# Banded attention on one Trainium2 core: normalising inside the split into two fp16 parts, tile by tile

## The chip, the cores and the metric

The program runs on one core of a Trainium2 chip. The metric is the device time of one execution in microseconds (us). In this text PE is TensorE's matmul and PEld its weight load, DVE is VectorE, ACT is ScalarE, POOL is GpSimd, and SP is the engine that issues the DMAs. "L335" is line 335 of the kernel before.

## What is computed

Three stages follow one another: an attention with a band of 128 keys and 4 "sink" keys, a feed-forward block with a three-tap convolution as its gate, and a mixing block with two token matrices. The change lies in the attention.

```python
scores = scale * np.matmul(q, k.transpose(0, 1, 3, 2))      # 2 batches, 8 heads, 768 x 768, head_dim 64
keep = is_sink | in_window                                  # 4 sinks, window 128
scores = np.where(keep, scores, -1000000000.0)
a = np.exp(scores - np.max(scores, axis=-1, keepdims=True))
a = a / (np.sum(a, axis=-1, keepdims=True) + 1e-09)
return np.matmul(a, v)
...
h = np.maximum(x @ w_in, 0.0)                               # d_model 512 -> d_ff 1024
gate = 1.0 / (1.0 + np.exp(-conv_out))                      # conv over 3 tokens
x = h * gate @ w_out
...
theta = x @ w_theta                                         # then cos, sin, two 768 x 768 token products
```

## The kernel before

**Units of work.** `body` walks through four units, one for each batch and half of the 768 query rows. A unit has four pairs of heads (`Unit.pair`), and each pair calls `head` twice. That makes 32 heads of three query tiles of 128 rows. For each tile TensorE multiplies queries and keys into PSUM (`scores`, tile `ps_s`, two buffers), VectorE adds the mask and takes the row maximum in one instruction (L315, into `e`), and ScalarE takes the exponential in place and sums it (L319). A tile of `e` is 260 columns wide: 128 keys, 4 sinks, 128 keys; the very first tile of a sequence is 128 wide. VectorE then forms the reciprocals `ri` of the three sums (L322, L323).

**Normalising and splitting.** Four heads (table `NORM`) are transposed by TensorE; the change does not touch them. The other 28 go this way. ScalarE multiplies each tile of `e` by its row factor, in place (L335). ScalarE copies the normalised blocks into fp16, the first part (L345), and VectorE subtracts that from `e` and writes the rest as a second fp16 part (L346); both go into the buffer `pb`, of which there are three. In a second half one instruction covers all three tiles (768 columns); in a first half the 128-wide tile goes alone and the other two together (512 columns). GpSimd splits the four sink columns in the same way (L349, L350). One transposing DMA, issued by SP, turns the head's parts into `pt` (L353), four buffers.

```python
for i in range(3):
    n = P if half == 0 and i == 0 else 2 * P + NS
    nc.scalar.activation(e[:, i, :n], e[:, i, :n], AF.Copy, scale=ri[:, i : i + 1])
```

**What uses it.** `pair_out` multiplies the parts in `pt` with the values, also split into two fp16 parts (`ps_o`, L411). It runs one head behind: `flush` comes after the next pair's first head. `store_x` scales the result and splits it again into `xg_hi` and `xg_lo` (L431, L432).

**What runs beside it.** Between the pairs `body` decodes the feed-forward weights (L100 to L103, L82, L84) and computes feed-forward blocks (`Group.blocks`), as the tables `CHUNKS` and `BLOCKS` say. A block is 24 matmuls into `ps_h` (L124 to L126), two ReLUs (L632), two first taps (L634), four further taps on VectorE (L636), one tanh (L640), a product (L641), a split into `ghi` and `glo` (L82, L84) and 12 matmuls into `ps_x` (L651, L652, L657). There are 24 such blocks; those that do not fit in the attention follow after it.

**What sets the order.** Each engine takes its instructions strictly in turn, and so does the DMA queue of SP. The order in these queues is written by the framework's scheduler when the program is built, from the instructions and their dependences; the tables only set the order in which they are handed to it.

Of the kernel before, what the change touches and what calls it, by code (L numbers as in the profile page):

```python
# [8 lines left out]
F32 = mybir.dt.float32  # L9
# [4 lines left out]
AF = mybir.ActivationFunctionType  # L14
ALU = mybir.AluOpType
PSUM = bass.MemoryType.PSUM

P = 128
B, H, S, D = 2, 8, 768, 64
NS = 4  # L20
SR = 3 * 3 * NS
KW = P + NS
# [23 lines left out]
RAW2 = 5  # L46
MIXED = (0, None, 1, None, None, None)
FLAG = 3
SK = 'gpsimd'
WT = 8  # L50
PRE_STACK = 1
TOK_CUT = 2
# [235 lines left out]
def scores(tc, c, half, qk, i, a):  # L288
    nc = tc.nc
    t = 3 * half + i  # L290
    ps = c.ps_s.tile([P, 512], F32, name="ps_s")
    o = KW * (max(t - 1, 0) - 2 * half)
    if len(qk) == 3:
        n = 2 * P + NS
        for k in qk[1:]:
            nc.tensor.matmul(ps[:, :n], qk[0][:, i * P : (i + 1) * P], k[:, o : o + n], start=k is qk[1], stop=k is qk[2])
        return ps
    n = P if t == 0 else 2 * P + NS
    nc.tensor.matmul(ps[:, :n], qk[0][:, a, i * P : (i + 1) * P], qk[1][:, o : o + n], start=True, stop=True)  # L299
    return ps  # L300


def head(tc, c, half, a, qk, norm):

    nc = tc.nc
    e = c.e.tile([P, 3, 2 * P + NS], F32, name="e")
    mx = c.st.tile([P, 3], F32, name="mx")
    sm = c.st.tile([P, 3], F32, name="sm")
    ri = c.st.tile([P, 3], F32, name="ri")
    for i in range(3):  # L310
        t = 3 * half + i
        n = P if t == 0 else 2 * P + NS
        ps = scores(tc, c, half, qk, i, a)
        m = c.masks[min(t, 2)]
        nc.vector.tensor_tensor_reduce(  # L315
            out=e[:, i, :n], in0=ps[:, :n], in1=m, scale=-1.0 / math.sqrt(D), scalar=3.0e38,
            op0=ALU.add, op1=ALU.min, accum_out=mx[:, i : i + 1],
        )
        nc.scalar.activation(  # L319
            e[:, i, :n], e[:, i, :n], AF.Exp, bias=mx[:, i : i + 1], scale=-1.0, accum_out=sm[:, i : i + 1]  # L320
        )
    nc.vector.tensor_scalar(sm, sm, 1.0e-9, 1.0 / SP, ALU.add, ALU.mult)  # L322
    nc.vector.reciprocal(ri, sm)  # L323
    c.last_sum = ri[:, 0:1]

    if norm == PE:
        return transposed_by_pe(tc, c, e, ri)
    nb = 5 if half == 0 else 6
    s0 = 2 if half == 0 else 0
    ns = 3 - s0  # L330
    pr = c.pbuf[c.npb % len(c.pbuf)]
    c.npb += 1
    for i in range(3):
        n = P if half == 0 and i == 0 else 2 * P + NS
        nc.scalar.activation(e[:, i, :n], e[:, i, :n], AF.Copy, scale=ri[:, i : i + 1])  # L335
    sk = e[:, s0:, P:KW]
    for i0, i1 in [(0, 3)] if half else [(0, 1), (1, 3)]:
        d0, d1 = max(2 * i0 - (1 - half), 0), 2 * i1 - (1 - half)
        hi, lo = pr[:, d0:d1, :], pr[:, nb + d0 : nb + d1, :]
        if d1 == 1:  # L340
            src, hi, lo = e[:, 0, :P], hi[:, 0, :], lo[:, 0, :]
        else:
            src = two_blocks(e, i0, i1 - i0)
            hi, lo = (x.rearrange("p (i w) q -> p i w q", w=2) for x in (hi, lo))
        nc.scalar.activation(hi, src, AF.Copy)  # L345
        nc.vector.tensor_tensor(lo, src, hi, ALU.subtract)  # L346

    ps = pr[:, 2 * nb, s0 * 3 * NS : SR].rearrange("p (i g w) -> p i g w", g=3, w=NS)
    getattr(nc, SK).tensor_copy(ps[:, :, 0:3:2, :], sk.unsqueeze(2).to_broadcast([P, ns, 2, NS]))  # L349
    getattr(nc, SK).tensor_tensor(ps[:, :, 1, :], sk, ps[:, :, 0, :], ALU.subtract)  # L350
    pt = c.pt.tile([P, 13, P], F16, name="pt")
    n = 2 * nb + 1
    nc.sync.dma_start_transpose(out=pt[:, :n, :], in_=pr[:, :n, :].rearrange("p a q -> p (a q)"))  # L353
    return pt


def transposed_by_pe(tc, c, e, ri):

    nc = tc.nc
    d = c.ma.tile([P, 3, P], F32, name="h")
    for i in range(3):
        nc.scalar.activation(d[:, i, :], c.ident, AF.Copy, scale=ri[:, i : i + 1])
    pt = c.pt.tile([P, 13, P], F16, name="pt")
    banks = c.ps_x.tile([P, DM], F32, name="ps_x"), c.ps_h.tile([P, 512], F32, name="ps_h")
    blocks = ((0, 0), (1, 0), (1, KW)), ((2, 0), (2, KW), (2, P))
    for n in range(2):
        for j, (i, k) in enumerate(blocks[n]):
            nc.tensor.matmul(banks[n][:, j * P : (j + 1) * P], e[:, i, k : k + P], d[:, i, :], start=True, stop=True)  # L370
        src = banks[n][:, : 3 * P]
        hi, lo = (pt[:, 6 * x + 3 * n : 6 * x + 3 * n + 3, :].rearrange("p a q -> p (a q)") for x in range(2))
        nc.scalar.activation(hi, src, AF.Copy)
        nc.vector.tensor_tensor(lo, src, hi, ALU.subtract)
    return pt


def two_blocks(e, i, n):

    a = e[:, i, 0 : 2 * P + NS]  # L380
    (pstep, pn), (step, _) = a.ap[0], a.ap[-1]
    return bass.AP(a.tensor, a.offset, [[pstep, pn], [(2 * P + NS) * step, n], [KW * step, 2], [step, P]])
# [65 lines left out]
class Unit:  # L448
# [11 lines left out]
    def pair(self, p):  # L460
        tc, c, b, half = self.tc, self.c, self.b, self.half
        n = (2 * b + half) * CC + p
        stack = n >= 3 * CC
        if not stack:
            while len(c.loaded) <= (n + AHEAD if n + AHEAD < 2 * CC else min(n + 1, 3 * CC - 1)):
                c.loaded.append(load_qk(tc, c, len(c.loaded)))
            qk = c.loaded[n]
        pts = []
        for a in range(2):
            if stack:  # L470
                while len(c.stacked) <= min(2 * n + a + 1, 8 * CC - 1):
                    c.stacked.append(load_stack(tc, c, len(c.stacked)))
                qk = c.stacked[2 * n + a]
            pts.append(head(tc, c, half, a, qk, NORM[n][a]))
            if n == 3 * CC - 1 and a == PRE_STACK:
                c.stacked.append(load_stack(tc, c, 3 * H))
            if a == LAG - 1:
                self.flush()
        while len(c.vp_t) <= min(p + V_AHEAD, CC - 1):
            c.vp_t.append(values(tc, c, b, len(c.vp_t)))  # L480
        c.late.append((b, p, half, pts, *c.vp_t[p]))
        if LAG == 0:
            self.flush()
# [507 lines left out]
```

## Time and profile before

| what | us |
|---|---|
| three runs | 475.7, 479.04, 496.11 |
| their median | 479.04 |
| the profiled execution, its own time | 475.81 |
| its span, first to last instruction | 474.0 |

A row of grouped instructions gives line, engine, operation, tiles (written<-read), shape and type, and the count; then the busy time in us and the mean duration of one in ns; then the idle time of the engine just before them and what ended it. Overlapping instructions count once in the busy time, so it can be less than count times mean. [...] A row of waits gives the engine and what it was to do, what ended the wait, the us in total, how often, and the longest. A row of the timeline gives start, length, engine, line, operation and, at its end, how many instructions it holds.

### The profile page before, as it was taken

To read this page: it belongs to the slowest core of one execution; us is meant where nothing else is said; L and a number is where in the kernel's file an instruction comes from. 1 tells how busy PE (TensorE), PEld (TensorE's weight loads), DVE (VectorE), ACT (ScalarE), POOL (GpSimd) and SP (SyncE) were. 2 spreads that over 40 slices of the span, in tenths; PEclk is the share of its full clock that TensorE was granted. 3 is DMA by queue.
4 is the path that set the end of the run, shared out by engine and by line. 5 is a ranking of instruction groups with operands and counts; after the bars stand their busy time and mean duration, and the time that the engine had idled before them with its cause. 6 is when DMAs were issued, how large, how long until landed. Compare 5 with 4: busy or idle time off the path is not lost.

```text
span 474.0 us, 7252 instructions
## 1 busy us (share of the span) xinstructions
PE 418.8 (88%) x2376; PEld 341.0 (72%) x2376; DVE 337.1 (71%) x870; ACT 316.2 (67%) x773; POOL 23.2 (5%) x92
## 2 busy tenths in 40 slices
PE   2877648797699899799999999899889999999994
PEld 1665336685488778688898888588668888888873
DVE  5689979997578997875699877897389973211132
ACT  2999869999999999985686877966475431100010
POOL 4101001010100101100000000000000000000000
PEclk9997778899979989899999999999989999999998
DMA  4888998567984665360434100131016730000012
GB/s 109 250 198 201 281 256 206 130 168 143 189 145 86 148 139 113 73 99 12 152 114 121 60 0 1 45 90 44 0 51 197 232 100 22 24 22 24 22 44 75
DMA packets 74589, 51.94 MB, mean 110 GB/s; under 512 B 59696, under 2 KB 63280, under 8 KB 74544
## 3 DMA queue, kind: packets, MB, share of 16 engines
q1 hardware_dynamic: 74544, 51.40, 43.6%
q8 instruction: 21, 0.34, 0.3%
q14 instruction: 24, 0.20, 0.1%
HBM read 33.95 MB, written 3.15 MB: 78 GB/s over the span
## 4 chain that ended last, share of the span: by engine, by line
PE 61%; ACT 15%; DVE 10%; DMA 9%; issue 3%; SPq 1%; POOL 0%; DVEq 0%; ACTq 0%
PE ps_y L125 7%; PE ps_y L124 7%; PE ps_y L126 7%; DMA pt<-pb 5%; PE ps_x L651 4%; PE ps_m L126 4%; PE ps_m L125 4%; PE ps_m L124 4%; PE ps_x L652 4%; PE ps_x L657 3%; PE ps_h L124 3%; PE ps_h L126 3%; PE ps_h L125 3%; ACT e L335 3%; ACT e L319 3%
## 5 line engine op out<-in xcount | busy, mean ns | idle before, releaser
L299 PE MATMUL ps_s<-qk 128*128 128x260 f32 (+1 forms) x144 | 48.7, 450 | 19.8 <-POOL sink_rows L221 8.7
L124 PE MATMUL ps_h<-xg_hi,win_hi 128*128 128x258 f32 x192 | 58.5, 306 | 1.8 <-ACT h L632 1.8
L124 PE MATMUL ps_y<-z_hi,wt_hi 128*128 128x512 f32 x144 | 57.6, 400 | 1.3 <-ACT z_hi L82 0.9
L125 PE MATMUL ps_y<-z_hi,wt_lo 128*128 128x512 f32 x144 | 57.0, 397 | 0.1
L126 PE MATMUL ps_y<-z_lo,wt_hi 128*128 128x512 f32 x144 | 56.4, 396 | 0.0
L125 PE MATMUL ps_h<-xg_hi,win_lo 128*128 128x258 f32 x192 | 55.9, 292 | 0.0
L126 PE MATMUL ps_h<-xg_lo,win_hi 128*128 128x258 f32 x192 | 55.7, 296 | 0.0
L82 ACT ACTIVATE xt_hi<-ps_t 128x512 fp32r<-128x512 f32 x24 | 13.9, 595 | 61.4 <-PE ps_t L685 61.4
L315 DVE CUSTOM_DVE_ANT_0 e<-ps_s,m 128x260 f32<-128x260 f32 (+1 forms) x96 | 37.6, 400 | 17.6 <-PE ps_s L299 12.1
L636 DVE SCALAR_TENSOR_TENSOR cv<-h,cw_t,cv 128x256 f32<-128x256 f32 x96 | 44.5, 480 | 7.4 <-ACT cv L634 6.8
L319 ACT ACTIVATE e<-e,mx 128x260 f32<-128x260 f32 (+1 forms) x96 | 47.7, 501 | 1.0 <-DVE mx L315 1.0
L299 PEld LDWEIGHTS ps_s<-qk 128*128 128x128 f32 x144 | 27.3, 226 | 28.9 <-DVE mx L315 12.0
L651 PE MATMUL ps_x<-wout_hi,ghi 128*128 128x512 f32 x96 | 41.3, 430 | 2.5 <-ACT ghi L82 2.5
L124 PEld LDWEIGHTS ps_h<-xg_hi,win_hi 128*128 128x128 f32 x192 | 38.2, 199 | 4.7 <-ACT h L632 2.6
L652 PE MATMUL ps_x<-wout_lo,ghi 128*128 128x512 f32 x96 | 40.1, 417 | 0.0
L753 DVE SCALAR_TENSOR_TENSOR slot<-ps_m,slot 128x512 f32<-128x512 f32 x12 | 8.3, 691 | 44.2 <-PE ps_m L126 44.2
L125 PEld LDWEIGHTS ps_h<-xg_hi,win_lo 128*128 128x128 f32 x192 | 38.2, 199 | 1.3
L126 PEld LDWEIGHTS ps_h<-xg_lo,win_hi 128*128 128x128 f32 x192 | 37.6, 198 | 0.9
L411 PE MATMUL ps_o<-pt,vp 128*64 128x256 f16 (+2 forms) x348 | 25.4, 268 | 13.7 <-DMA pt<-pb 11.7
L335 ACT ACTIVATE e<-e,ri 128x260 f32<-128x260 f32 (+1 forms) x84 | 36.1, 508 | 0.0
L411 PEld LDWEIGHTS <-vp 128*64 128x64 f16 (+1 forms) x348 | 18.8, 116 | 23.5 <-issue 14.9
L124 PEld LDWEIGHTS ps_y<-z_hi,wt_hi 128*128 128x128 f32 x144 | 27.1, 188 | 8.0 <-ACT z_hi L82 1.2
(146 smaller groups left out, 984.6 us busy)
## 6 DMA issues: line engine op xcount, KB each, us to landing
raw<-in_w_tok_r_dram SPq DMA_DIRECT2D x12, 384.0 KB, 3.2
raw<-in_w_tok_i_dram SPq DMA_DIRECT2D x12, 384.0 KB, 3.2
slot<-in_w_in_dram SPq DMA_DIRECT2D x8, 512.0 KB, 6.1
slot<-in_w_out_dram SPq DMA_DIRECT2D x8, 512.0 KB, 4.8
qk<-in_q_dram SPq DMA_DIRECT2D x32, 96.0 KB, 2.7
slot<-in_vt_dram SPq DMA_DIRECT2D x8, 384.0 KB, 3.7
out_dram<-slot SPq DMA_DIRECT2D x12, 256.0 KB, 2.0
raw<-in_w_theta_dram SPq DMA_DIRECT2D x8, 256.0 KB, 3.0
```

The lines of the kernel that those rows point to most:

```text
L124: nc.tensor.matmul(out, whi, xhi, start=first, stop=False)
L125: nc.tensor.matmul(out, wlo, xhi, start=False, stop=False)
L126: nc.tensor.matmul(out, whi, xlo, start=False, stop=last)
L299: nc.tensor.matmul(ps[:, :n], qk[0][:, a, i * P : (i + 1) * P], qk[1][:, o : o + n], start=True, stop=True)
L315: nc.vector.tensor_tensor_reduce(out=e[:, i, :n], in0=ps[:, :n], in1=m, scale=-1.0 / math.sqrt(D), scalar=3.0e38, op0=ALU.add, op1=ALU.min ...
L319: nc.scalar.activation(e[:, i, :n], e[:, i, :n], AF.Exp, bias=mx[:, i : i + 1], scale=-1.0, accum_out=sm[:, i : i + 1])
L335: nc.scalar.activation(e[:, i, :n], e[:, i, :n], AF.Copy, scale=ri[:, i : i + 1])
L411: nc.tensor.matmul(po[a * D : (a + 1) * D, q], w[:, a * D : (a + 1) * D], pts[a][: w.shape[0], b0:b1, :], start=(n == 0), stop=(n == len(j ...
L636: nc.vector.scalar_tensor_tensor(cv[:, n, :], h[:, n, k : GT + k], w[:, k : k + 1], cv[:, n, :], ALU.mult, ALU.add)
L651: nc.tensor.matmul(self.px[t], ghi[:, n, s], whi, start=f2 == 0 and n == 0, stop=False)
L652: nc.tensor.matmul(self.px[t], ghi[:, n, s], wlo, start=False, stop=False)
L657: nc.tensor.matmul(self.px[t], glo[:, n, s], whi, start=False, stop=f2 == FB // 2 - 1 and n == 1)
```

## The change

ScalarE's in-place normalisation is gone. Its scaled copy now writes the first fp16 part directly, from the not yet normalised `e`, one instruction for each query tile. VectorE's subtraction becomes a multiply-and-subtract that applies the same row factor, also one for each tile. GpSimd gets a multiplication of its own for the sink columns, into a small new tile `sk` (four buffers), since `e` is no longer normalised. The name `SK` goes; the engine it named, GpSimd, stays.

```diff
-SK = 'gpsimd'
...
+
+    sk = c.st.tile([P, 3, NS], F32, name="sk")[:, s0:, :]
+    nc.gpsimd.tensor_tensor(sk, e[:, s0:, P:KW], ri[:, s0:].unsqueeze(2).to_broadcast([P, ns, NS]), ALU.mult)
     for i in range(3):
-        n = P if half == 0 and i == 0 else 2 * P + NS
-        nc.scalar.activation(e[:, i, :n], e[:, i, :n], AF.Copy, scale=ri[:, i : i + 1])
-    sk = e[:, s0:, P:KW]
-    for i0, i1 in [(0, 3)] if half else [(0, 1), (1, 3)]:
-        d0, d1 = max(2 * i0 - (1 - half), 0), 2 * i1 - (1 - half)
-        hi, lo = pr[:, d0:d1, :], pr[:, nb + d0 : nb + d1, :]
-        if d1 == 1:
-            src, hi, lo = e[:, 0, :P], hi[:, 0, :], lo[:, 0, :]
-        else:
-            src = two_blocks(e, i0, i1 - i0)
-            hi, lo = (x.rearrange("p (i w) q -> p i w q", w=2) for x in (hi, lo))
-        nc.scalar.activation(hi, src, AF.Copy)
-        nc.vector.tensor_tensor(lo, src, hi, ALU.subtract)
+        first = half == 0 and i == 0
+        d0, d1 = (0, 1) if first else (2 * i - (1 - half), 2 * i + 1 + half)
+        src = e[:, i, :P].unsqueeze(1) if first else two_blocks(e, i, 1)[:, 0]
+        hi, lo, r = pr[:, d0:d1, :], pr[:, nb + d0 : nb + d1, :], ri[:, i : i + 1]
+        nc.scalar.activation(hi, src, AF.Copy, scale=r)
+        nc.vector.scalar_tensor_tensor(lo, src, r, hi, ALU.mult, ALU.subtract)
 
     ps = pr[:, 2 * nb, s0 * 3 * NS : SR].rearrange("p (i g w) -> p i g w", g=3, w=NS)
-    getattr(nc, SK).tensor_copy(ps[:, :, 0:3:2, :], sk.unsqueeze(2).to_broadcast([P, ns, 2, NS]))
-    getattr(nc, SK).tensor_tensor(ps[:, :, 1, :], sk, ps[:, :, 0, :], ALU.subtract)
+    nc.gpsimd.tensor_copy(ps[:, :, 0:3:2, :], sk.unsqueeze(2).to_broadcast([P, ns, 2, NS]))
+    nc.gpsimd.tensor_tensor(ps[:, :, 1, :], sk, ps[:, :, 0, :], ALU.subtract)
```

Since lines fall away, the changed kernel's numbers are lower by one ahead of this place and by five behind it: L345 and L346 become L340 and L341, the blocks' L632, L634, L636 and L640 become L627, L629, L631 and L635.

ScalarE's queue in the middle of the attention, where the third head of the second unit is written to the buffer `pb_200` (`win_hi`, `wout_hi` and `dec_t` belong to the decoding of weights, `h` and `cv` to feed-forward blocks), before:

```order
L335 ACTIVATE e<-e,ri 128x260 x3
L319 ACTIVATE e,sm<-e,mx 128x260
L632 ACTIVATE h<-ps_h 128x258
L100 ACTIVATE dec_t<-slot_118 128x512
L632 ACTIVATE h<-ps_h 128x258
L82 ACTIVATE win_hi<-slot_116 128x512
L345 ACTIVATE pb_200<-e 128x768
```

and the same head now:

```order
L426 ACTIVATE xg_hi<-ps_o,vst 128x129
L340 ACTIVATE pb_200<-e,ri 128x256 x3
L318 ACTIVATE e,sm<-e,mx 128x260
L81 ACTIVATE win_hi<-slot_115 128x512
L627 ACTIVATE h<-ps_h 128x258
```

Three passes and a fourth over the same head, with five other instructions between them, have become three passes in a row.

VectorE's queue at the same head, before:

```order
L84 TENSOR_TENSOR win_lo<-slot_116,win_hi 128x512
L323 RECIPROCAL ri<-sm 128x3
L346 TENSOR_TENSOR pb_200<-e,pb_200 128x768
L636 SCALAR_TENSOR_TENSOR cv<-h,cw_t,cv 128x256
L102 SCALAR_TENSOR_TENSOR slot_118<-dec_t,slot_118 128x512
```

and now:

```order
L341 SCALAR_TENSOR_TENSOR pb_200<-e,ri,pb_200 128x256
L631 SCALAR_TENSOR_TENSOR cv<-h,cw_t,cv 128x256
L341 SCALAR_TENSOR_TENSOR pb_200<-e,ri,pb_200 128x256
L101 SCALAR_TENSOR_TENSOR slot_114<-dec_t,slot_114 128x512
L341 SCALAR_TENSOR_TENSOR pb_200<-e,ri,pb_200 128x256
L631 SCALAR_TENSOR_TENSOR cv<-h,cw_t,cv 128x256
```

One subtraction has become three, with a convolution tap and a decoding step between them.

ScalarE's queue at the end of the attention, around the last head's first part (the table load prepares the sine functions of the next stage), before:

```order
L82 ACTIVATE ghi<-cv 128x512
L632 ACTIVATE h<-ps_h 128x258
L640 ACTIVATE cv<-cv 128x512
L335 ACTIVATE e<-e,ri 128x260 x3
L834 ACT_TABLE_LOAD
L834 ACTIVATE scratch<-ri 128x1
L632 ACTIVATE h<-ps_h 128x258
L634 ACTIVATE cv<-h,cw_t 128x256
L345 ACTIVATE pb_200<-e 128x768
```

and now:

```order
L627 ACTIVATE h<-ps_h 128x258
L659 ACTIVATE slot_118<-ps_x 128x512
L318 ACTIVATE e,sm<-e,mx 128x260
L659 ACTIVATE slot_118<-ps_x 128x512
L629 ACTIVATE cv<-h,cw_t 128x256
L318 ACTIVATE e,sm<-e,mx 128x260
L635 ACTIVATE cv<-cv 128x512
L340 ACTIVATE pb_200<-e,ri 128x256 x3
```

The table load has moved behind the last head, and a further feed-forward group's copies out of `ps_x` (L659, formerly L664) have moved ahead of it. Ahead of the last head's first part ScalarE's queue holds 12 tanh instructions of feed-forward blocks before and 14 now.

## Rows read from the trace of the kernel before

**Rows 1.** Busy time by windows of the span: attention, and what follows.

```profile
10.00:70.00 60.00, 42.00 (x238) 30.38 (x238) 50.37 (x172) 52.23 (x150) 6.02 (x26) 0.84 0.92 234
70.00:110.00 40.00, 35.43 (x228) 29.00 (x224) 37.66 (x104) 38.23 (x99) 4.52 (x14) 0.90 0.68 168
110.00:160.00 50.00, 42.95 (x321) 35.01 (x319) 36.10 (x134) 49.16 (x146) 4.39 (x20) 0.93 0.76 142
160.00:210.00 50.00, 44.96 (x329) 38.07 (x326) 42.55 (x121) 49.97 (x133) 4.85 (x18) 0.93 0.56 113
210.00:300.00 90.00, 89.92 (x550) 78.06 (x549) 69.59 (x139) 63.55 (x134) 0.00 (x0) 1.00 0.23 64
```

**Rows 2.** ScalarE's instructions grouped by line and shape, window 70 to 210 us.

```profile
L335 ACT ACTIVATE e<-e,ri 128x260 f32<-128x260 f32 x61 | 27.4, 529 | 0.0
...
L634 ACT ACTIVATE cv<-h,cw_t 128x256 f32<-128x256 f32 x26 | 13.0, 525 | 0.0
L345 ACT ACTIVATE pb<-e 128x768 f16<-128x768 f32 x15 | 13.0, 864 | 0.0
L632 ACT ACTIVATE h<-ps_h 128x258 f32<-128x258 f32 x26 | 10.0, 396 | 0.3 <-PE ps_h L126 0.3
L640 ACT ACTIVATE cv<-cv 128x512 f32<-128x512 f32 x12 | 7.8, 654 | 0.0
L82 ACT ACTIVATE ghi<-cv 128x512 fp32r<-128x512 f32 x12 | 7.7, 643 | 0.0
...
L345 ACT ACTIVATE pb<-e 128x512 f16<-128x512 f32 x8 | 5.0, 628 | 0.0
...
L345 ACT ACTIVATE pb<-e 128x128 f16<-128x128 f32 x8 | 2.4, 306 | 0.0
L664 ACT ACTIVATE slot<-ps_x 128x512 f32<-128x512 f32 x4 | 2.3, 608 | 0.0
```

**Rows 3.** ScalarE's timeline around two heads of the attention.

```profile
110.79 1.30 ACT L335 ACTIVATE e<-e,ri 128x260 f32<-128x260 f32 x3
...
115.10 0.83 ACT L345 ACTIVATE pb<-e 128x768 f16<-128x768 f32 x1
115.83 0.92 ACT L207 ACTIVATE slot<-slot,vst 128x768 f16<-128x768 f32 x1
```

**Rows 4.** VectorE's instructions grouped by line and shape, window 70 to 210 us.

```profile
L636 DVE SCALAR_TENSOR_TENSOR cv<-h,cw_t,cv 128x256 f32<-128x256 f32 x50 | 23.2, 478 | 3.7 <-ACT cv L634 3.5
L315 DVE CUSTOM_DVE_ANT_0 e<-ps_s,m 128x260 f32<-128x260 f32 x55 | 23.1, 423 | 9.7 <-PE ps_s L299 5.8 <-PE ps_s L296 2.8 <-DVE pb L346 0.5
L346 DVE TENSOR_TENSOR pb<-e,pb 128x768 f16<-128x768 f32 x15 | 14.2, 946 | 1.4 <-ACT pb L345 1.4
...
L84 DVE TENSOR_TENSOR glo<-cv,ghi 128x512 fp32r<-128x512 f32 x11 | 7.5, 681 | 0.4 <-ACT ghi L82 0.4
L346 DVE TENSOR_TENSOR pb<-e,pb 128x512 f16<-128x512 f32 x8 | 5.5, 685 | 0.0
...
L432 DVE SCALAR_TENSOR_TENSOR xg_lo<-ps_o,vst,xg_hi 128x129 fp32r<-128x129 f32 x11 | 3.8, 346 | 1.0 <-ACT xg_hi L431 1.0
...
L346 DVE TENSOR_TENSOR pb<-e,pb 128x128 f16<-128x128 f32 x8 | 2.3, 285 | 0.0
```

**Rows 5.** TensorE's timeline inside feed-forward blocks, behind the attention.

```profile
241.86 0.28 PE L124 MATMUL ps_h<-xg_hi,win_hi 128*128 128x258 f32 x1
...
244.04 1.09 PE L657 MATMUL ps_x<-wout_hi,glo 128*128 128x512 f32 x4
```

**Rows 6.** Waits over the whole run.

```profile
PEld ps_s L299 <- DVE mx L315: 12.0, 14, 3.4
PE ps_o L411 <- DMA pt<-pb: 11.7, 9, 4.7
```

**Rows 7.** The buffer `pb`: count, shortest, median and longest duration (ns), whole run.

```profile
L349 POOL CAST pb<-e x28: 189/203/767, 37.1 to 206.5; 128x24 f16<-128x24 f32 x16, 128x8 f16<-128x8 f32 x12
L350 POOL TENSOR_TENSOR pb<-e,pb x28: 198/208/532, 37.8 to 206.8; 128x12 f16<-128x12 f32 x16, 128x4 f16<-128x4 f32 x12
```

## The prediction

> **What bounds the kernel now.** I read the windows first [rows 1]. From 210 us on TensorE is busy 89.92 of 90 us: behind the attention it is the limit, and the work it has left there sets the end. In the attention it is not. From 10 to 70 us the DMA engines are in use 0.92 of the time and the granted clock is 0.84; this stretch is held by its transfers. From 70 to 210 us, three windows, the sums are ScalarE 38.23 + 49.16 + 49.97 = 137.4 of 140 us (98%), TensorE 123.3 (88%), VectorE 116.3 (83%). So ScalarE sets the pace of this stretch. But VectorE is close: from 70 to 110 us it has 37.66 of 40 us (94%), and there both are full. What the change is worth is read from 70 to 210 us. A faster attention shortens the run only as far as TensorE gets rid of idle time there, 16.7 us in all.
>
> Next the groups of ScalarE and VectorE in that stretch [rows 2, 4], for the prices; then ScalarE's timeline, for how far instructions overlap [rows 3]; then the waits [rows 6].
>
> **ScalarE.** In this stretch 69 tiles are normalised (61 of 260 columns, 8 of 128) and 31 copies make the first parts: 15 of 768, 8 of 512 and 8 of 128 columns, 13.0 + 5.0 + 2.4 = 20.4 us [rows 2]. The copies go. The 69 scaled passes stay, with 256 columns instead of 260 and fp16 output. A scaled pass of 256 columns takes 525 ns (L634), one of 260 takes 529 (L335), so I price this at no change. A lower end comes from the fp16 copies: between 306 ns at 128 and 628 at 512 columns, 256 would take 413, and 61 x 0.116 = 7 us more would be saved; the upper end is 529. I take the scaled pass, since it has the same row factor. Neighbours on ScalarE overlap: the 768-wide copy lasts 0.83 us but the next instruction starts 0.73 after it [rows 3]. The 31 copies therefore free 20.4 - 31 x 0.10 = 17.3 us.
>
> **VectorE.** The subtractions of the same heads go: 14.2 + 5.5 + 2.3 = 22.0 us [rows 4]. Instead come 61 multiply-and-subtracts of 256 columns and 8 of 128. The same operation with a row factor takes 478 ns at 256 columns (L636) and 346 at 129 (L432): 61 x 0.478 + 8 x 0.346 = 31.9 us. VectorE gains 9.9 us of work. The lower end takes the plain subtraction's slope, 285 ns at 128 and 685 at 512, hence 418 at 256: 27.8 us, plus 5.8. The upper end is the row factor's price. I take that, because L636 is the same operation. Splitting one wide instruction into three is what costs here.
>
> [...]
>
> **GpSimd** gets 28 multiplications in all; its nearest is the subtraction of sink columns, 208 ns in the median and 532 at the longest [rows 7], so 6 us, 15 at worst. It is busy 13.8 of these 140 us [rows 1], so its own idle time hides them. If that cover went, the transposing DMA would start up to 0.5 us later for a head. The multiplication needs only `e` and `ri`, so it no longer waits for L335.
>
> **Waits.** A head's parts are ready sooner: three passes 1.30, copy 0.73 and subtraction 0.95 us follow one another now [rows 3, 4]; afterwards three passes and one multiply-and-subtract, 1.30 + 0.48, about 1.2 us less. TensorE waits for transposes in 9 places, 11.7 us over the run [rows 6]. The values' matmuls run a head behind, so what a transpose waits for is mostly the queue; I count 0, the other end is the gain 9 x 1.2 = 11 us. VectorE waits for a first part 84 times over the run where it did 40 times; in the stretch the old wait cost 1.4 us [rows 4]. Behind such an instruction queue the next row maxima, which free `ps_s` for TensorE's scores; TensorE's loads wait 12.0 us over the run for those already [rows 6]. ScalarE issues a head's three passes in a row (order above), so I count 0 here too; the other end is one pass of 0.53 us for each of 23 heads, 12 us.
>
> **What moves.** The scheduler filled the time it sees on ScalarE: 14 tanh stand ahead of the last first part where 12 did (order above), so two feed-forward blocks are brought forward. On TensorE a block is 24 matmuls at (244.04 - 241.86)/18 = 0.12 us and 12 at 0.23 (four last 1.09, one 0.39 of it behind the last start) [rows 5], 5.7 us, and two are 11.4 us that no longer stand behind the attention. In the attention they cost VectorE two products and two splits at 0.68 and six taps at 0.478, 5.6 us [rows 4]. They cost ScalarE two tanh, two splits, two ReLUs, three taps and two copies out of `ps_x`: 1.3 + 1.3 + 0.8 + 1.6 + 1.2 = 6.2 us, and with 0.1 of overlap each 5.1.
>
> **Sum.** The stretch of 140 us would hold ScalarE 137.4 - 17.3 + 5.1 = 125.2, VectorE 116.3 + 9.9 + 5.6 = 131.8, TensorE 123.3 + 11.4 = 134.7 us. All three become nearly equal, so none can run at 98%. VectorE's best share in this stretch is 94% [rows 1], which asks for 131.8/0.94 = 140.2 us; TensorE's best is 44.96 of 50, 90%, which asks for 149.7. I take the middle, 145: the attention gets 5 us longer, with 11.4 us more of TensorE's work done in it. Net 6.4 us. From 10 to 70 us I count nothing, since the transfers stay. The profiled execution took 475.81 us (span 474.0 and 1.8 around it), so I predict 469.4, 1.3% less. The median of the runs shown, 479.04, is 3.2 above the profiled execution; against it this is 2.0%.
>
> **Rivals.**
> *All of it fits.* The stretch stays at 140 us: 475.8 - 11.4 = 464.4. For it: first parts come sooner, and TensorE's granted clock of 0.90 to 0.93 in these windows could rise with less idling. Against: TensorE at 134.7 of 140 us, 96%, which it reaches in no window of the attention.
> *VectorE becomes the bound (slower).* Its idle time comes from waiting for scores (9.7 us before L315) and first parts [rows 4], and these waits stay as work is added. At today's share of 83% the stretch takes 131.8/0.83 = 158.8 us, and the time is 475.8 + 18.8 - 11.4 = 483.2; with the 84 waits at their upper end 12 us more, 495. It decides when VectorE's share stays under 131.8/151.4 = 87%, for then the longer stretch outweighs the 11.4 us. Against: with ScalarE relieved, those who made VectorE wait are earlier.
> *TensorE keeps its share.* The blocks moved forward merely push scores and values back, at 88%: 134.7/0.88 = 153 us, net 475.8 + 13 - 11.4 = 477.4; the change gives nothing.
> *GpSimd gets in VectorE's way.* A cast of 24 columns takes 203 ns in the median and up to 767 [rows 7]: one of the two engines makes the other wait. If VectorE is the one, 23 multiplications of 208 to 532 ns cost it 5 to 12 us, it asks for 146 to 153 us, and the middle with TensorE's 149.7 gives 472 to 476. [...]
>
> **How the numbers follow.** Forecast 0.40 (its own range 463 to 475), all fits 0.20, VectorE the bound 0.23, TensorE's share 0.12, GpSimd 0.05. The range that leaves out 2 in 10 runs from 460, the first rival with a little of the transposes' gain, to 488, VectorE's rival with a part of the added waits. About 2% is what a measurement of this kernel can tell from no change: 466.3 to 485.3. Faster: all of the first rival and 0.13 of the forecast, 0.33. Slower: 0.17 of VectorE's rival and 0.02 of TensorE's, 0.19. The rest, 0.48, is within 2%.
>
> **What would show it.** Right: no in-place normalisation on ScalarE, 72 scaled first parts near 525 ns, 72 multiply-and-subtracts near 478 ns, ScalarE's share from 70 to 210 us down to 85 to 90%, VectorE's up to 90%, TensorE's to 92 or 93%, and the last first part at 205 to 220 us with 14 tanh ahead of it. The step on prices is wrong if the new instructions are off by over 50 ns. The step on shares is wrong if VectorE stays below 87% while its waits for first parts or scores grow, or if TensorE's wait for row maxima grows beyond 12 us; then the time is above 475.8.

## The result, and the profile after

The changed kernel takes 464.03 us in the median of 4 runs (462.15 to 465.06). The kernel before, run beside it, takes 479.95 us in the median of 4 (475.7 to 496.11). The ratio of the two means, 0.9693 with a 95% interval from 0.9614 to 0.9771, leaves out the slow run of 496.11 us: about 3% faster. The forecast was 469.4 us in a range from 460 to 488. Its mechanism was only partly right, and the first rival, *All of it fits* with 464.4 us, came nearest.

The profiled execution of the changed kernel took 464.74 us, its span is 462.7 us. Busy time by windows. A row gives start and end, the length, busy time and (count) for PE, PEld, DVE, ACT and POOL, TensorE's granted clock as a share of full, the mean share of the 16 DMA engines in use, and GB/s, here as in [rows 1]:

```profile
10.00:70.00 60.00, 41.56 (x238) 30.75 (x239) 50.50 (x179) 50.87 (x146) 9.39 (x34) 0.85 0.94 235
70.00:110.00 40.00, 32.39 (x213) 25.55 (x208) 37.43 (x105) 30.95 (x82) 5.87 (x16) 0.89 0.59 153
110.00:160.00 50.00, 45.30 (x347) 36.87 (x348) 44.29 (x169) 48.67 (x148) 9.08 (x34) 1.00 0.89 170
160.00:210.00 50.00, 49.63 (x379) 43.11 (x379) 45.86 (x134) 46.00 (x125) 8.61 (x23) 1.00 0.48 96
210.00:300.00 90.00, 87.40 (x519) 74.82 (x518) 73.10 (x146) 65.65 (x138) 0.00 (x0) 1.00 0.25 72
```

From 70 to 210 us ScalarE is busy 125.6 us (137.4 before), VectorE 127.6 (116.3) and TensorE 127.3 (123.3). TensorE started 939 matmuls in these three windows; before it was 878. From 10 to 70 us the DMA engines are in use 0.94 of the time (0.92 before); as in the forecast, I read this stretch as held by its transfers.

Read the clock column next. In steps of half a microsecond the kernel before shows 0.50 from 130 to 135.5 us and 1.00 from 136 us on; between these two levels only steps in which it changes show other values. So a mean of 0.90 over 40 us is 8 us at 0.50. By that reading the kernel before spends 8 + 7 + 7 = 22 us of the three windows at the lower level [rows 1], and the changed one 8.8, all of it ahead of 110 us. At that level matmuls take nearly twice as long: in the kernel before those into `ps_h` start 0.22 us apart from 134.19 to 135.49 us, at 0.50, and 0.12 apart from 136.06 us on, at 1.00. So some of TensorE's busy time did no more than stretch. With half of the slow time taken off, which is an estimate that counts TensorE as busy all through it, TensorE did 123.3 - 11.0 = 112.3 us of full-clock work in this stretch before, and 127.3 - 4.4 = 122.9 after. That is 10.6 us more, close to the whole gain. A count that needs no clock agrees: by 210 us TensorE had started 377 matmuls into `ps_h` and 180 into `ps_x`, before it was 336 and 155, and at 0.12 and 0.23 us each the difference is 10.7 us.

The totals of the run say the same. Each kernel's profile page, engines' busy time, first before and then after:

```profile
PE 418.8 (88%) x2376; PEld 341.0 (72%) x2376; DVE 337.1 (71%) x870; ACT 316.2 (67%) x773; POOL 23.2 (5%) x92
```

```profile
PE 410.3 (89%) x2376; PEld 334.6 (72%) x2376; DVE 341.9 (74%) x914; ACT 297.1 (64%) x733; POOL 36.4 (8%) x120
```

The same 2376 matmuls take TensorE 8.5 us less, and its idle time fell only from 55.2 to 52.4 us. Together these are the 11.3 us by which the span is shorter. By this account three quarters of it are matmuls that stretched less, but the account does not make the clock the cause. Five executions of the kernel before had a mean granted clock of 0.962 or 0.963, where the two profiled executions have 0.949 before and 0.965 after, and still took 476.4 to 477.4 us; two at 0.938 took 478.6 and 479.3. In the old order a clock higher by 0.025, by the same reckoning 12 us of stretch, went with a run about 2 us shorter. So the higher clock alone brings little; in the changed kernel it comes together with the work brought forward.

The prices come from the groups by line and shape, 70 to 210 us of the changed kernel, which answer to [rows 2, 4]; the last two lines are from its view of the buffer `pb`, which answers to [rows 7]:

```profile
L340 ACT ACTIVATE pb<-e,ri 128x256 f16<-128x256 f32 x58 | 25.6, 509 | 0.1
...
L340 ACT ACTIVATE pb<-e,ri 128x128 f16<-128x128 f32 x8 | 3.2, 397 | 0.1
```

```profile
L341 DVE SCALAR_TENSOR_TENSOR pb<-e,ri,pb 128x256 f16<-128x256 f32 x58 | 26.0, 479 | 0.2
...
L314 DVE CUSTOM_DVE_ANT_0 e<-ps_s,m 128x260 f32<-128x260 f32 x54 | 22.7, 423 | 6.4 <-PE ps_s L298 4.6 <-PE ps_s L295 1.4
...
L341 DVE SCALAR_TENSOR_TENSOR pb<-e,ri,pb 128x128 f16<-128x128 f32 x8 | 2.8, 347 | 0.0
```

```profile
L341 DVE SCALAR_TENSOR_TENSOR pb<-e,ri,pb x84: 320/478/486, 39.1 to 207.9; 128x256 f16<-128x256 f32 x72, 128x128 f16<-128x128 f32 x12
L344 POOL CAST pb<-sk x28: 189/268/1207, 34.1 to 206.3; 128x24 f16<-128x24 f32 x16, 128x8 f16<-128x8 f32 x12
```

A first part takes 509 ns and a multiply-and-subtract 479, as foreseen. VectorE stands idle 0.2 us in all ahead of its wide multiply-and-subtracts; ahead of the wide subtractions it was 1.4. The last second part starts at 207.9 us, where it was 209.6 in the kernel before:

```profile
L346 DVE TENSOR_TENSOR pb<-e,pb x40: 280/685/959, 42.5 to 209.6; 128x768 f16<-128x768 f32 x16, 128x128 f16<-128x128 f32 x12, 128x512 f16<-128x512 f32 x12
```

Waits of the changed kernel over its whole run, which answer to [rows 6]:

```profile
PE ps_o L406 <- DMA pt<-pb: 9.4, 11, 2.5
...
PEld ps_s L298 <- DVE mx L314: 6.1, 11, 2.2
PE ps_x L646 <- ACT ghi L81: 5.9, 6, 2.5
```

TensorE's loads wait 6.1 us for row maxima instead of 12.0, and its matmuls 9.4 us for transposes instead of 11.7.

### The profile page after: what moved, and what is told of

Its sections match the earlier page's. It is cut to its first block, busy times and chain, and to the rows that moved or that the text cites. A ratio compares the mean times of both kernels' runs of the same rounds, so it can differ in the third digit from the quotient of the medians.

```text
span 462.7 us, 7296 instructions
## 1 busy us (share of the span) xinstructions
PE 410.3 (89%) x2376; PEld 334.6 (72%) x2376; DVE 341.9 (74%) x914; ACT 297.1 (64%) x733; POOL 36.4 (8%) x120
## 4 chain that ended last, share of the span: by engine, by line
PE 63%; DMA 14%; ACT 9%; DVE 9%; issue 2%; SPq 1%; ACTq 0%; DVEq 0%
PE ps_y L125 7%; PE ps_y L124 7%; PE ps_y L123 7%; PE ps_x L646 4%; DMA pt<-pb 4%; PE ps_m L123 4%; PE ps_m L125 4%; PE ps_m L124 4%; PE ps_x L647 4%; PE ps_x L652 4%; PE ps_h L123 3%; DMA vp<-slot 3%; PE ps_h L124 3%; PE ps_h L125 3%; PE ps_o L406 3%; DMA slot<-in_vt_dram 3%
## 5 line engine op out<-in xcount | busy, mean ns | idle before, releaser
L123 PE MATMUL ps_h<-xg_hi,win_hi 128*128 128x258 f32 x192 | 57.3, 300 | 1.2 <-ACT xg_hi L426 1.2
L298 PE MATMUL ps_s<-qk 128*128 128x260 f32 (+1 forms) x144 | 46.5, 436 | 12.3 <-DVE par_flag L151 8.7
L125 PE MATMUL ps_h<-xg_lo,win_hi 128*128 128x258 f32 x192 | 54.6, 290 | 0.0
L314 DVE CUSTOM_DVE_ANT_0 e<-ps_s,m 128x260 f32<-128x260 f32 (+1 forms) x96 | 37.7, 400 | 14.5 <-PE ps_s L298 11.0
L631 DVE SCALAR_TENSOR_TENSOR cv<-h,cw_t,cv 128x256 f32<-128x256 f32 x96 | 44.6, 479 | 3.2 <-ACT cv L629 2.8
L646 PE MATMUL ps_x<-wout_hi,ghi 128*128 128x512 f32 x96 | 40.1, 418 | 5.9 <-ACT ghi L81 5.9
L123 PEld LDWEIGHTS ps_h<-xg_hi,win_hi 128*128 128x128 f32 x192 | 37.1, 194 | 3.5 <-ACT xg_hi L426 1.6
L124 PEld LDWEIGHTS ps_h<-xg_hi,win_lo 128*128 128x128 f32 x192 | 37.2, 194 | 2.4 <-DVE win_lo L83 1.1
L647 PE MATMUL ps_x<-wout_lo,ghi 128*128 128x512 f32 x96 | 38.8, 404 | 0.0
L341 DVE SCALAR_TENSOR_TENSOR pb<-e,ri,pb 128x256 f16<-128x256 f32 (+1 forms) x84 | 35.9, 459 | 0.2
L340 ACT ACTIVATE pb<-e,ri 128x256 f16<-128x256 f32 (+1 forms) x84 | 35.4, 491 | 0.2
```

The costliest lines, as they stand in the source:

```text
L123: nc.tensor.matmul(out, whi, xhi, start=first, stop=False)
L124: nc.tensor.matmul(out, wlo, xhi, start=False, stop=False)
L125: nc.tensor.matmul(out, whi, xlo, start=False, stop=last)
L314: nc.vector.tensor_tensor_reduce(out=e[:, i, :n], in0=ps[:, :n], in1=m, scale=-1.0 / math.sqrt(D), scalar=3.0e38, op0=ALU.add, op1=ALU.min ...
L340: nc.scalar.activation(hi, src, AF.Copy, scale=r)
L341: nc.vector.scalar_tensor_tensor(lo, src, r, hi, ALU.mult, ALU.subtract)
```

## The experiments

The theory from the forecast: ScalarE sets the pace of the attention, and 17 us taken off it let the scheduler bring feed-forward work forward. The rivals: the gain is the order of the queues alone; VectorE or GpSimd matter; it is the clock. Each kernel was timed beside the kernel before, whose medians there were 478.38, 477.4 and 478.56 us; the changed kernel was not timed again there. "Work" is TensorE's full-clock work from 70 to 210 us, worked out as above from each run's own windows.

| kernel | us | ratio, 95% interval | ScalarE busy, 70 to 210 us | work |
|---|---|---|---|---|
| before | 478.4 | 1 | 137.4 | 112.3 |
| after | 464.0 | 0.969 [0.961, 0.977] | 125.6 | 122.9 |
| e1, VectorE's half alone | 478.3 | 1.001 [0.997, 1.004] | 134.0 | 114.4 |
| e2, ScalarE's half alone | 470.1 | 0.983 [0.978, 0.988] | 124.9 | 118.1 |
| e7, tiles without the factor | 474.0 | 0.992 [0.989, 0.995] | 124.1 | 117.9 |
| e3, change, copies put back | 473.3 | 0.991 [0.987, 0.995] | 131.4 | 109.2 |
| e4, change, no product on GpSimd | 463.8 | 0.970 [0.965, 0.975] | 124.9 | 121.3 |
| e5, change, tiles backwards | 468.6 | 0.982 [0.976, 0.987] | 123.8 | 116.7 |
| e10, before, tiles backwards | 477.7 | 0.999 [0.995, 1.003] | 128.5 | 107.5 |
| e6, change in 20 of 28 heads | 474.5 | 0.994 [0.991, 0.998] | 124.4 | 114.2 |
| e13, change, more blocks early | 470.4 | 0.985 [0.979, 0.990] | 121.9 | 121.4 |
| e14, before, more blocks early | 479.5 | 1.003 [1.000, 1.007] | 136.2 | 112.9 |
| e11, change, dearer first parts | 478.6 | 1.001 [0.997, 1.004] | 123.7 | 110.9 |
| e12, before, dearer normalisation | 478.1 | 0.999 [0.996, 1.003] | 135.7 | 109.9 |

### The halves of the change

VectorE's half alone (e1): the kernel before, its subtraction split into three with a factor of one.

```diff
-        nc.vector.tensor_tensor(lo, src, hi, ALU.subtract)
+    for i in range(3):
...
+        nc.vector.scalar_tensor_tensor(pr[:, nb + d0 : nb + d1, :], src, c.one, pr[:, d0:d1, :], ALU.mult, ALU.subtract)
```

> ScalarE does what it did before (in-place normalisation and wide copies); VectorE's second parts are written as in the change, 84 multiply-and-subtracts one tile at a time, the factor being a column of ones. The scheduler puts 14 tanh ahead of the last first part, as in the change. Theory 'ScalarE sets the pace': ScalarE stays near 98% from 70 to 210 us, no gain, 476 to 484 us (ratio to before 0.995 to 1.02). Rival 'the order alone' (blocks brought forward bring the gain): 465 to 468 us (0.97 to 0.98). Rival 'VectorE is the bound as soon as it has 10 us more': above 486 us (over 1.02).

Measured 478.32 us, ratio 1.0005. VectorE's group in e1, 70 to 210 us:

```profile
L350 DVE SCALAR_TENSOR_TENSOR pb<-e,one,pb 128x256 f16<-128x256 f32 x52 | 22.2, 479 | 1.8 <-ACT pb L345 1.7
```

VectorE pays the price of the change, 479 ns a tile, and the run is not slower for it. Nor is it faster, although 14 tanh instructions stand ahead of the last first part in e1, as many as in the changed kernel.

ScalarE's half alone (e2): the changed kernel with VectorE's old wide subtraction, which leaves the row factor out of the second part.

```diff
         nc.scalar.activation(hi, src, AF.Copy, scale=r)
-        nc.vector.scalar_tensor_tensor(lo, src, r, hi, ALU.mult, ALU.subtract)
+    for i0, i1 in [(0, 3)] if half else [(0, 1), (1, 3)]:
...
+        nc.vector.tensor_tensor(lo, src, hi, ALU.subtract)
```

> ScalarE as in the change; VectorE subtracts as before, one wide instruction over several tiles, so the factor is left out of the second part. VectorE has about 12 us less to do than in the change. The scheduler puts 11 tanh ahead of the last first part. Theory 'ScalarE sets the pace' and TensorE is the next limit: 461 to 465 us, about as the change (ratio 0.96 to 0.972). Rival 'VectorE bounds the change': 452 to 458 us (0.945 to 0.957). Rival 'the order alone': with fewer blocks ahead than before, 474 us or more (0.99 or more).

Measured 470.08 us, ratio 0.9832, between what the theory and the order alone had foreseen. Then the same with one plain subtraction for each tile (e7):

```diff
-        nc.vector.scalar_tensor_tensor(lo, src, r, hi, ALU.mult, ALU.subtract)
+        nc.vector.tensor_tensor(lo, src, hi, ALU.subtract)
```

> The change with VectorE's second parts as plain subtractions, still one tile at a time (418 ns estimated from the slope of L346 instead of 478; the factor is left out of the second part). 11 tanh ahead of the last first part, as in the run with one wide subtraction, which took 470.1 us. Theory 'tile-wise second parts shorten the wait of the transposes': 461 to 466 us. Rival 'the order made the wide run slower': 468 to 472 us.

Measured 474.04 us, ratio 0.9918, above both ranges. The view of `pb` in e7 has the price of the plain subtraction, 418 ns in the median:

```profile
L341 DVE TENSOR_TENSOR pb<-e,pb x84: 263/418/439, 37.1 to 200.3; 128x256 f16<-128x256 f32 x72, 128x128 f16<-128x128 f32 x12
```

Both give VectorE less to do than the change does, 120.1 and 119.0 us in the stretch instead of 127.6, and both are slower than the change. So nothing here says that VectorE's share limited the changed kernel. ScalarE's half brings 8 us in e2 and 3 in e7, with the same work taken off ScalarE. So ScalarE's load alone does not set the time; the two differ in the cut of the subtraction and in the order of the queues.

### ScalarE's load put back

The changed kernel with 40 wide copies on ScalarE, written to a spare tile (e3):

```diff
+    for i0, i1 in [(0, 3)] if half else [(0, 1), (1, 3)]:
...
+        nc.scalar.activation(hi, src, AF.Copy)
```

> The change, and ScalarE also does the 40 wide fp16 copies of before, into a spare buffer that nobody reads. VectorE as in the change. 13 tanh ahead of the last first part. Theory 'ScalarE sets the pace': ScalarE is back at 97% or more from 70 to 210 us, and the time is that of before or a little more, 474 to 484 us (ratio 0.99 to 1.015). Rival 'shorter chain from the sums to the transposing DMA' (the copies are off that chain): 464 to 468 us. Rival 'the order alone': 468 to 471 us.

Measured 473.25 us, ratio 0.9907: two thirds of the gain are gone, and the time lies just below the theory's range. By the time the mixing stage starts its token products (`ps_y`), all of the gain is gone. Their first matmul starts at 299.5 us in the kernel before, at 287.7 in the changed one and at 303.7 in e3:

```profile
L124 PE MATMUL ps_y<-z_hi,wt_hi x144: 388/394/503, 299.5 to 453.6; 128*128 128x512 f32 x144
```

```profile
L123 PE MATMUL ps_y<-z_hi,wt_hi x144: 387/394/502, 287.7 to 441.1; 128*128 128x512 f32 x144
```

```profile
L123 PE MATMUL ps_y<-z_hi,wt_hi x144: 388/395/495, 303.7 to 449.8; 128*128 128x512 f32 x144
```

There e3 is 4 us behind the kernel before, with as much of the product with `w_theta` done ahead of it (72 matmuls into `ps_m`; 60 in the changed kernel). What it still gains, it gains behind that place, where the edit changes no instruction. By itself this speaks for ScalarE's load. The copies are off the way from the sums to the transposing DMA, so in this order a shorter way there does not carry the gain.

### GpSimd's product left out

```diff
-    sk = c.st.tile([P, 3, NS], F32, name="sk")[:, s0:, :]
-    nc.gpsimd.tensor_tensor(sk, e[:, s0:, P:KW], ri[:, s0:].unsqueeze(2).to_broadcast([P, ns, NS]), ALU.mult)
+    sk = e[:, s0:, P:KW]
```

> The change without GpSimd's multiplication: the sink columns are split unnormalised. The order on TensorE, ScalarE, VectorE and SP is the same as in the change, instruction by instruction. Theory 'GpSimd is hidden': 462 to 466 us, as the change, within 0.4%. Rival 'GpSimd gets in VectorE's way': 6 us or more are freed, 455 to 460 us (ratio 0.95 to 0.96).

Measured 463.77 us, 0.3 below the changed kernel. The other engines' queues have the same order here, so this is the one clean subtraction of the study: the product costs nothing that these runs can tell, since single runs of either kernel lie up to 3 us apart.

### Order alone

The tile loop backwards, in the changed kernel (e5) and in the normalisation of the kernel before (e10):

```diff
-    for i in range(3):
+    for i in (2, 1, 0):
```

> The change with its loop over the three tiles run backwards (third tile first). The same instructions; the scheduler gives TensorE, ScalarE and VectorE another order, with 11 tanh ahead of the last first part instead of 14. Theory 'work taken off ScalarE brings the gain': 463 to 470 us (ratio to before 0.967 to 0.981). Rival 'the order alone': 474 us or more (0.99 or more).

> The kernel before with its loop of normalisations run backwards. The same instructions in another order, with 13 tanh ahead of the last first part instead of 12. Theory 'work taken off ScalarE brings the gain': no gain here, 474 to 482 us (ratio 0.99 to 1.008). Rival 'the order alone': a reordering can give as much as the change did, 464 to 469 us (0.97 to 0.98).

Measured 468.57 us for e5 and 477.71 for e10, both in the range of the theory. Neither adds an instruction or takes one away. The changed kernel loses 4.5 us by it; the kernel before loses and gains nothing. In e5, too, the first matmul into `ps_y` starts late, at 298.1 us: of the 6.8 us by which its profiled execution is shorter than that of the kernel before (spans of 467.2 and 474.0) 5.4 lie behind that place.

The change with 8 heads of the second unit left in the old form (e6):

```diff
+    if c.wide_heads(c.npb - 1):
...
+            nc.scalar.activation(hi, src, AF.Copy)
+            nc.vector.tensor_tensor(lo, src, hi, ALU.subtract)
+    else:
...
```

> The form of before for the eight heads of the second unit (70 to 110 us, where VectorE was the fuller engine before and ScalarE has 9 us to spare in the change), the form of the change for the other 20. Theory 'each stretch by its fuller engine': TensorE gets back some of the 3 us that it lost from 70 to 110 us, 460 to 464 us (ratio 0.96 to 0.97). Rival 'ScalarE is still the pace there': eight wide copies come back, 6 us of ScalarE, 466 to 470 us.

Measured 474.45 us, ratio 0.9941, above both ranges. With the change in 20 of 28 heads, a gain in proportion to the work would be 20/28 of 14 us, 10; 3 came. ScalarE's load does not add up head by head.

Last, the table of blocks, in the changed kernel (e13) and in the one before (e14):

```diff
-BLOCKS = ((0, 0, 0, 0), (1, 0, 0, 0), (0, 1, 1, 2), (1, 4, 3, 2))
+BLOCKS = ((0, 0, 0, 0), (1, 0, 0, 0), (0, 1, 1, 2), (2, 4, 4, 1))
```

> The change, with the feed-forward blocks of the fourth unit handed to the scheduler as 2, 4, 4, 1 instead of 1, 4, 3, 2: 15 tanh ahead of the last first part instead of 14. More of the feed-forward work fits into the attention: one block is 5.7 us of TensorE, so 458 to 462 us. The attention is full with 14, and a further block makes it longer by as much: 463 to 468 us. An order that starves TensorE somewhere would give 468 to 472.

> The kernel before with the same table of blocks, 2, 4, 4, 1: 12 tanh ahead of the last first part, as before. If order and table alone can give what the change gave, 464 to 470 us. If the kernel before is held by ScalarE in the attention, nothing is to be had from them: 475 to 480 us.

Measured 470.38 us for e13, where an order that starves TensorE had been put, and 479.47 for e14. No version was clearly faster than the changed kernel. In e13 ScalarE writes the last head's first parts at 221.19 us:

```profile
221.19 1.31 ACT L340 ACTIVATE pb<-e,ri 128x256 f16<-128x256 f32 x3
```

in the changed kernel at 206.42:

```profile
206.42 1.29 ACT L340 ACTIVATE pb<-e,ri 128x256 f16<-128x256 f32 x3
```

With a fifteenth tanh ahead of that place the attention is 14.8 us longer, for one block more of 5.7 us. In this order the fifteenth did not fit; whether another order has room for it was not tried.

### ScalarE made dearer

In the changed kernel (e11), and in the same way in L335 of the kernel before (e12), each pass uses `Identity` in place of `Copy` and reads a bias of zero from memory:

```diff
-        nc.scalar.activation(hi, src, AF.Copy, scale=r)
+        nc.scalar.activation(hi, src, AF.Identity, bias=c.zero, scale=r)
```

> The change, with ScalarE's 84 first parts made a little dearer: the pass takes a bias of zero from memory as well, which changes no value. I estimate about 0.09 us more each, 7 us over the run; the trace will give the price. ScalarE is still the pace of the changed kernel: the whole 7 us come back, 471 to 474 us. ScalarE now has room, and the work taken off it has stopped mattering: 464 to 468 us. The scheduler writes another order for it too, which in the runs so far has moved the changed form by up to 5 us from 464 to 469.

> The kernel before, with the same zero bias on its 84 in-place normalisations. ScalarE sets the pace of the kernel before: the 7 us that I estimate for it appear in the time, 482 to 486 us. TensorE's waits and the clock set it, and ScalarE's load is no more than a neighbour: 476 to 480 us. If the changed kernel with the same bias loses clearly less than this one, ScalarE's load has been the bound before and has ceased to be it.

Measured 478.56 us for e11 and 478.13 for e12. The prices, from ScalarE's groups from 70 to 210 us, first of e11 and then of e12:

```profile
L340 ACT ACTIVATE pb<-e,zero,ri 128x256 f16<-128x256 f32 x55 | 29.2, 595 | 0.0
```

```profile
L335 ACT ACTIVATE e<-e,zero,ri 128x260 f32<-128x260 f32 x55 | 30.3, 624 | 0.0
```

Against 509 and 529 ns that is 86 and 95 ns more each (the 0.09 us expected was my estimate, from no row), over 84 passes at most 7.2 and 8.0 us. The kernel before lost none of its 8.0, which is hard to square with a ScalarE that sets the pace. The changed kernel lost 14.5, twice the price of what was added. e12 lies where the rival had put it; e11 lies above both ranges.

Where e11 lost it, TensorE's windows show. Busy time in steps of 10 us, first of e11 and then of the changed kernel:

```profile
130.00:140.00 10.00, 7.36 (x74) 6.29 (x71) 7.89 (x28) 10.00 (x28) 1.83 (x7) 0.95 0.93 189
140.00:150.00 10.00, 9.92 (x59) 8.03 (x58) 7.74 (x28) 9.06 (x28) 1.39 (x6) 0.88 0.26 54
...
180.00:190.00 10.00, 4.18 (x32) 3.49 (x32) 9.61 (x30) 10.00 (x28) 1.99 (x5) 0.84 0.45 85
190.00:200.00 10.00, 10.00 (x66) 8.25 (x62) 8.22 (x23) 6.71 (x15) 1.28 (x4) 0.82 0.68 129
```

```profile
120.00:130.00 10.00, 8.37 (x71) 6.24 (x69) 7.24 (x34) 9.81 (x32) 0.92 (x5) 1.00 1.03 189
130.00:140.00 10.00, 9.25 (x75) 7.72 (x75) 8.01 (x36) 10.00 (x32) 2.25 (x9) 1.00 0.85 164
...
180.00:190.00 10.00, 10.00 (x64) 8.77 (x63) 9.47 (x31) 9.81 (x28) 2.65 (x6) 1.00 0.36 80
```

In e11 TensorE stands still for 5.8 of the 10 us from 180. Its timeline there names the waits in brackets:

```profile
181.68 0.63 PE L295 MATMUL ps_s<-stack,stack 128*128 128x260 f32 x4
182.98 0.24 PE L406 MATMUL ps_o<-pt,vp 128*64 128x128 f16 x1 [0.67 <-DMA pt<-pb]
183.16 0.51 PE L295 MATMUL ps_s<-stack,stack 128*128 128x260 f32 x2
186.11 0.51 PE L295 MATMUL ps_s<-stack,stack 128*128 128x260 f32 x2 [2.44 <-DVE mx L314]
189.33 2.08 PE L406 MATMUL ps_o<-pt,vp 128*64 128x128 f16 x23 [2.71 <-DMA pt<-pb]
```

and TensorE's timeline in the changed kernel, among its scores of that time:

```profile
183.63 0.40 PE L295 MATMUL ps_s<-stack,stack 128*128 128x260 f32 x2
...
184.11 0.40 PE L295 MATMUL ps_s<-stack,stack 128*128 128x260 f32 x2
...
187.42 1.10 PE L652 MATMUL ps_x<-wout_hi,glo 128*128 128x512 f32 x4
188.36 0.40 PE L295 MATMUL ps_s<-stack,stack 128*128 128x260 f32 x2
```

In e11 scores and values stand one behind the other in TensorE's queue, and each waits for VectorE or a transpose with nothing to do meanwhile. In the changed kernel four microseconds of feed-forward matmuls stand between two sets of scores, from 184.35 to 188.36 us, so the row maxima are there when their turn comes. Apart from the dearer passes the engines do the same work; what stands beside a wait differs.

## Why the prediction was right or wrong

The time lies in the range of 28 us, but the likeliest outcome of the forecast, a change within 2% at 0.48, did not come; faster, which came, had 0.33.

**ScalarE's terms** held. No normalisation in place is left, a first part takes 509 ns where 525 to 529 were priced, and ScalarE's share from 70 to 210 us fell to 90%, the upper edge of the 85 to 90 foreseen.

**VectorE's price** held: 479 ns for 478, 347 for 346. The plain subtraction of e7 took 418, the lower end that the forecast read from the slope of L346; the form with a row factor is 61 ns above that, so its own row, L636, was the better guide. VectorE's sum was too high all the same: 131.8 us foreseen, 127.6 measured. Over the whole run its busy time rose by 4.8 us (337.1 to 341.9), in e1 by 5.2, where the prices of 84 narrow instructions less those of 40 wide ones make about 12. Neighbours overlap on VectorE too, which the forecast allowed for on ScalarE only: in the changed kernel's timeline three such instructions of 0.47 to 0.48 us start 0.40 us apart.

```profile
162.99 0.48 DVE L341 SCALAR_TENSOR_TENSOR pb<-e,ri,pb 128x256 f16<-128x256 f32 x1
163.39 0.47 DVE L631 SCALAR_TENSOR_TENSOR cv<-h,cw_t,cv 128x256 f32<-128x256 f32 x1
163.79 0.47 DVE L341 SCALAR_TENSOR_TENSOR pb<-e,ri,pb 128x256 f16<-128x256 f32 x1
```

**GpSimd and the added waits** were rightly counted at nothing. e4 puts the product at 0.3 us. In the row of L341 the longest of 84 is 486 ns with a median of 478, while GpSimd's cast was stretched to 1207 ns. The timeline has that cast beside two VectorE instructions that are no longer than elsewhere, where their groups have means of 681 and 686 ns:

```profile
94.69 0.67 DVE L102 SCALAR_TENSOR_TENSOR slot<-slot 128x512 int32<-128x512 int32 x1
94.83 1.21 POOL L344 CAST pb<-sk 128x24 f16<-128x24 f32 x1
95.29 0.67 DVE L636 SCALAR_TENSOR_TENSOR cv<-cv,h 128x512 f32<-128x512 f32 x1
```

The cast ends 0.08 us behind the second of them. Here GpSimd was the one that waited; of a VectorE that waits for GpSimd these rows show nothing.

**TensorE's wait for row maxima** did not grow; it halved. VectorE had been waiting for first parts and scores before, and is 91% busy now without being late, so *VectorE becomes the bound* fell, and e1 shows it in the kernel before as well. TensorE's own share came to 91%, just under the 92 or 93 foreseen.

**What failed is the step "TensorE's best is 44.96 of 50, 90%, which asks for 149.7. I take the middle, 145".** The attention did not get 5 us longer; its last second part starts at 207.9 us instead of 209.6. TensorE reached 49.63 of 50 us from 160 to 210. And the 134.7 us that I laid on it were not there: I had added 11.4 us to a busy time of which some 11 were matmuls stretched by the lower clock. TensorE paused for 12.7 us instead of 16.7, 13.2 of the 22 slow us went, and its busy time came out at 127.3. The last matmul into `ps_h` shows the net, in TensorE's timeline before

```profile
287.42 0.28 PE L126 MATMUL ps_h<-xg_lo,win_hi 128*128 128x258 f32 x1
```

and after:

```profile
275.01 0.28 PE L125 MATMUL ps_h<-xg_lo,win_hi 128*128 128x258 f32 x1
```

12.4 us earlier, against 11.4 for two blocks that are done sooner at no cost in length. That is the first rival's number. It had named first parts that come sooner, and the clock; the clock did rise, but the executions of the kernel before show that this alone is worth little.

The 11.4 us themselves came true by some luck. They were read from two tanh more in the queue, and e1 has the same two and no gain. With the loop backwards the same change takes 468.6 us, close to the forecast of 469.4; which order the scheduler would write was not foreseen.

**What the runs took from the theory.** "ScalarE sets the pace of this stretch" was too simple. 8 us more on ScalarE cost the kernel before nothing (e12), and 14 tanh ahead of the last first part go with 464 us in the changed kernel and with 478 in e1, so that count is no measure of the gain. On the other hand, with the old load on ScalarE five orders of the queues (before, e1, e10, e12, e14) all lie between 477.4 and 479.5 us, and only e3 falls below, at 473.3. With the lighter load seven orders (after, which e4 shares, e5, e13, e2, e7, e6, e11) lie between 464 and 478.6, on average 471.4. As a rough estimate from these few orders, room on ScalarE is thus worth some 6 to 7 us on average, and the order that the scheduler happened to write about another 7 to the changed kernel. Six of the lighter kernels, and none of the others, gave TensorE more than 116 us of full-clock work in the stretch. That work is not all of it either: in the five orders with the old load it goes from 107.5 to 114.4 us while their times stay within 2 us.

**What stays open.** Except for e4 every edit also moved the order, so the price of ScalarE's load in a fixed order was not measured. For e11 the order is shown as the place of a 5.8 us loss, not as the whole of its 14.5. What holds the orders with the old load near 478 us, if 8 us more on ScalarE cost nothing there, is not shown. Nor is it shown why e3 and e5 gain behind the start of the token products.

## What to carry to other kernels

Where a scheduler writes the queues, one time of one build measures the change and one draw of the order together: try a few edits that keep the work and shake the order (a loop backwards is enough) before crediting the change. When adding work to an engine whose granted clock is below full, estimate the stretched part of its busy time and take it off first: here it was some 11.0 of TensorE's 123.3 us, and 6.6 of them went while its pauses fell from 16.7 to 12.7 us. And in strict queues look at what stands beside a wait: an engine with independent work between two dependent steps can spend the wait on that, as TensorE did with four microseconds of feed-forward matmuls in the changed kernel, where e11 waited 2.44 us for row maxima.

## What the runs showed of the hardware that was not expected

In windows of 10 us from 10 to 210 us, over all fourteen kernels, 123 have a granted clock under 1.00; in each of them, or in the window ahead of it, TensorE was busy for at most 8.23 us. So each fall of the clock there had a pause of TensorE in or ahead of it. The windows before, 110 to 170 us:

```profile
110.00:120.00 10.00, 7.07 (x54) 5.24 (x53) 6.53 (x24) 10.00 (x26) 1.70 (x6) 1.00 0.95 161
120.00:130.00 10.00, 6.17 (x56) 4.43 (x55) 5.67 (x30) 9.48 (x33) 0.78 (x4) 0.96 0.92 192
130.00:140.00 10.00, 9.72 (x62) 7.90 (x60) 8.21 (x28) 10.00 (x31) 0.40 (x3) 0.70 0.95 144
...
160.00:170.00 10.00, 7.65 (x40) 6.21 (x37) 9.78 (x30) 10.00 (x28) 1.34 (x4) 0.83 0.67 157
```

Two windows with pauses, busy 7.07 and 6.17 of 10 us, then 0.70 while TensorE is busy 9.72: the lower clock came after the pauses here. A pause did not always bring a fall: e13 was busy 7.75 of 10 us from 220 and kept 1.00:

```profile
220.00:230.00 10.00, 7.75 (x62) 6.38 (x60) 3.89 (x9) 6.17 (x13) 1.24 (x3) 1.00 0.23 43
```

With `Identity` and a zero bias read from memory in place of `Copy`, a ScalarE pass of 256 columns took 86 ns more, and one of 260 columns 95, in the rows of e11 and e12; the two parts of that edit were not taken apart.
